# Seam copies ahead of filter units, three fillers fewer, and a gate on one filter load, in a fused Fourier filter and SwiGLU kernel

## The chip, the core, the metric

One core of one Trainium2 chip. The metric is the device time in microseconds (us) of one execution. The kernel before takes 893.56 us (median of 4 runs, 893.45 to 894.48). Ratios below are the mean time of one kernel's runs over that of the other's runs of the same rounds, so they are not quite the ratio of the medians quoted beside them. Later rounds add 40 runs of the kernel before, on the chips of the experiments (892.24 to 898.20).

Engines: PE (matrix multiply; PEld is its weight load), DVE (vector), ACT (scalar), POOL (GpSimd), SP (issues transfers). A "slot" below is one step of the main loop, one of 12 hidden blocks of one group of up to 512 tokens: gate and value matmuls, silu, product, and the down-projection of the block two slots earlier. There are 588. A "filler" is a matmul on zeros whose result nobody uses; a "bank" is one of the buffers (PSUM) into which PE writes and from which the other engines copy; the "opening" is all that comes before the first gate matmul. A "seam" is the slot in which the down-projection of one group ends.

## The reference, cut to what matters

```python
def _attn_ref(x, filt_r, filt_i):          # x: 8 x 3008 x 256
    X = np.fft.rfft(x, axis=1)
    F = (filt_r + 1j * filt_i)[None, :, :]
    return np.fft.irfft(X * F, n=x.shape[1], axis=1)

def _moe_ref(x, w_gate, w_val, w_out, rms_g):   # 24064 tokens, 256 -> 1536 -> 256
    xn = x / rms * rms_g
    g = xn @ w_gate
    return (g * sigmoid(g) * (xn @ w_val)) @ w_out
```

The transform over 3008 = 47 x 64 positions is done with matmuls in two stages, A and B; after stage B the spectrum is multiplied by the real and the imaginary filters; two inverse stages and a norm follow. Batch 0 is transformed in the opening, before the main loop; the other batches' transforms are woven into the main loop, slot by slot.

## The kernel before: the parts concerned

The filters come in four chunks, real (fr) and imaginary (fi). Each chunk is loaded into half of the partitions (f_load) and then copied to the other half (f_dup, by ACT or POOL, in one case by a transfer). The opening, with cuts:

```python
        for c in range(4):
            f_load(c, 0, nc.sync)
            f_load(c, 1, nc.gpsimd if c < 3 else nc.sync)

        warm_up(14, 1)                      # fillers: matmuls on zeros
        for g in range(4):
            wi_group(g)                     # tables for the inverse stage
        for m in range(6):                  # stage A of batch 0
            if m == 4:
                warm_up(6, 0)
            for dh in range(2):
                at_unit(m, dh)
            for g in ((4, 5), (6,), (), (), (7,), ())[m]:
                wi_group(g)
            if m == 4:
                warm_up(3, 0)
        warm_up(2, 0)
        ...
        for g in range(4):
            t1_mm(g)
            t1_copy(g, g == 1)              # token copies: ACT if true, else DVE
        stage_b(0, 1, 2, 3)
        for g in range(4, 8):
            t1_mm(g)
        f_dup(0, 0, A, 0, 2)                # chunk, real/imaginary, engine, rows
        f_dup(0, 1, G, 0, 2)
        f_dup(0, 0, A, 2, 4)
        f_dup(0, 1, G, 2, 8)
        t1_copy(4, 1)
        f_dup(0, 0, A, 4, 8)
        products(0)
        ...
        f_dup(1, 1, G)                      # POOL: the second imaginary chunk
        products(3)                         # POOL's first product, next in its order
```

The main loop emits, per slot, the gate and value matmuls, then the planned units of the next batches, then the down-projection, whose last block ends with the copy of the accumulators (two banks) to SBUF (the seam copy, half on ACT, half on DVE):

```python
        def at(slot, fn, *a):
            todo = {q_unit: late, swap_unit: pre}.get(fn, plan).setdefault(slot, [])
        ...
        for i in range(len(items) + 4):
            for fn, a in pre.get(i, ()):
                fn(*a)
            if i < len(items):
                gv(*items[i])
            for fn, a in plan.get(i, ()):
                fn(*a)
            if 2 <= i < len(items) + 2:
                down(*items[i - 2])         # at i mod 12 = 1: ends with the seam copies
            ...
            for fn, a in late.get(i, ()):
                fn(*a)
```

## Time and profile before

| | before |
|---|---|
| time, median of 4 | 893.56 us |
| span of the profiled execution | 890.6 us |
| PE busy | 873.5 us (98%) |
| first gate matmul (end of the opening) | 47.15 us |
| main loop, from there to the end | 843.45 us |
| visible PE waits in the main loop | 4.3 us |

The lines that carry this are shown in the prediction. One more follows: POOL in the opening of the kernel before. The columns are start, length in us, engine, line, what is written from what, and in brackets the idle time before it and what ended it.

```profile
23.24 1.89 POOL L520 COPY fi<-fi 64x2048 f32<-64x2048 f32 x1 [1.39 <-DMA fi<-in_filt_i_dram]
25.94 1.27 POOL L268 TENSOR_TENSOR sg<-v,fr 128x512 f16<-128x512 f32 x1 [0.81 <-ACT v L266]
27.19 1.26 POOL L269 TENSOR_TENSOR hh<-v,fi 128x512 f16<-128x512 f32 x1
28.51 1.89 POOL L520 COPY fi<-fi 64x2048 f32<-64x2048 f32 x1
30.48 1.27 POOL L268 TENSOR_TENSOR sg<-v,fr 128x512 f16<-128x512 f32 x1
```

The first line is the copy of the second imaginary chunk, which waits for its transfer. After the next wait, for ACT, POOL runs without a gap.

### The profile page before, as it was taken

The numbers are of one execution on the slowest core, as the hardware profiler recorded it, in microseconds if no ns is written. First come the engines' busy times: TensorE is split into PE (matmuls) and PEld (weight loads), VectorE is DVE, ScalarE is ACT, GpSimd is POOL, SyncE is SP. The second block draws the span as 40 slices with busy tenths as digits, with TensorE's granted clock in tenths as the row PEclk, the third lists the DMA queues.
The fourth block names the chain that finished last, engine by engine and source line by source line (L and its number), as shares of the span: only waits on it lengthen the run. The fifth ranks groups of instructions, "written<-read, shape, count | busy, mean of one in ns | idle before, by whom it ended". The sixth has DMA issues, their size and how long they took to land.

```text
span 890.6 us, 17468 instructions
## 1 busy us (share of the span) xinstructions
PE 873.5 (98%) x6258; PEld 559.4 (63%) x6258; DVE 681.5 (77%) x1091; ACT 625.1 (70%) x1068; POOL 435.6 (49%) x392
## 2 busy tenths in 40 slices
PE   8799999999999999999999999999999999999997
PEld 5666666666666666666666666666666666666556
DVE  7866787889987877888688787888878887555555
ACT  7877657677677766877677766787657765676444
POOL 7843830656427661677236662376515762155300
PEclk9999999999999999999999999999999999999999
DMA  8696726675663456335645247233352232222202
GB/s 196 122 196 156 157 67 207 143 158 110 162 159 89 101 111 185 107 90 113 159 119 132 86 81 199 80 94 90 88 163 72 67 90 61 85 66 49 72 24 48
DMA packets 80095, 101.44 MB, mean 114 GB/s; under 512 B 8108, under 2 KB 56684, under 8 KB 79560
## 3 DMA queue, kind: packets, MB, share of 16 engines
q1 hardware_dynamic: 69688, 84.23, 34.8%
q0 software_dynamic: 10240, 15.96, 11.4%
q8 instruction: 49, 0.80, 0.4%
q14 instruction: 38, 0.31, 0.1%
q10 hardware_dynamic: 80, 0.13, 0.1%
HBM read 67.67 MB, written 46.78 MB: 129 GB/s over the span
## 4 chain that ended last, share of the span: by engine, by line
PE 87%; issue 4%; DVE 2%; ACT 2%; DMA 2%; POOL 2%; SPq 0%; ACTq 0%; POOLq 0%; DVEq 0%
PE po L462 26%; PE pg L443 25%; PE pv L443 25%; PE psi L291 3%; PE psb L238 3%; PE psn L323 2%; PE psa L203 2%; DMA fr<-in_filt_r_dram 1%; DVE o L469 1%; ACT fr L516 1%; DVE hh L448 1%; DMA rb<-r_tmp 1%; ACT gT L578 1%; PE psq L352 0%; POOL xc L188 0%
## 5 line engine op out<-in xcount | busy, mean ns | idle before, releaser
L448 DVE TENSOR_TENSOR hh<-pv,sg 128x512 f16<-128x512 f32 (+2 forms) x588 | 392.9, 670 | 190.2 <-ACT sg L447 77.6
L447 ACT ACTIVATE sg<-pg 128x512 f16<-128x512 f32 (+2 forms) x588 | 340.9, 580 | 227.5 <-PE pg L443 217.8
L462 PE MATMUL po<-wo,hh 128*128 128x256 f16 x2244 | 343.2, 272 | 3.8 <-DVE o L469 3.0
L443 PE MATMUL pv<-xn,wv 128*128 128x512 f16 (+2 forms) x1176 | 339.6, 370 | 0.0
L443 PE MATMUL pg<-xn,wg 128*128 128x512 f16 (+2 forms) x1176 | 339.5, 370 | 0.0
L462 PEld LDWEIGHTS <-hh 128*128 128x128 f16 x2256 | 216.4, 98 | 99.0 <-issue 5.3
L282 POOL TENSOR_TENSOR s<-s,s 128x512 f16<-128x512 f16 x102 | 117.9, 1157 | 237.5 <-DVE s L276 165.6
L443 PEld LDWEIGHTS <-wv 128*128 128x128 f16 x1176 | 114.9, 98 | 128.8 <-issue 0.3
L419 POOL TENSOR_TENSOR xn<-y,rb 128x1024 f16<-128x1024 f32 (+1 forms) x45 | 126.0, 2801 | 44.9 <-DMA rb<-r_tmp 37.7
L443 PEld LDWEIGHTS <-wg 128*128 128x128 f16 x1176 | 111.4, 98 | 13.0 <-issue 0.3
L358 POOL TENSOR_TENSOR rho<-u,mhalf 128x4 f32<-128x4 f32 (+1 forms) x48 | 49.1, 1022 | 63.5 <-DVE u L356 63.1
L276 DVE TENSOR_TENSOR s<-psb,fi 64x512 f16<-64x512 f32 x102 | 69.8, 684 | 3.1
L296 ACT ACTIVATE t<-psi 96x512 f16<-96x512 f32 x112 | 66.4, 593 | 8.1 <-PE psi L291 2.7
L278 DVE SCALAR_TENSOR_TENSOR s<-psb,fi 64x512 f16<-64x512 f32 x102 | 70.7, 693 | 1.4
L252 DVE TENSOR_TENSOR s<-psb,fr 128x512 f16<-128x512 f32 x102 | 69.4, 681 | 0.0
L329 ACT ACTIVATE y<-psn,gsb 128x512 f32<-128x512 f32 (+1 forms) x94 | 63.8, 679 | 7.8 <-PE psn L323 0.5
L343 POOL TENSOR_TENSOR sq<-sq 128x512 f16<-128x512 f16 (+1 forms) x35 | 39.6, 1133 | 35.9 <-ACT sq L335 35.9
L335 ACT ACTIVATE sq<-psn 128x512 f16<-128x512 f32 (+1 forms) x94 | 54.8, 583 | 0.0
L208 ACT ACTIVATE t<-psa 128x512 f16<-128x512 f32 x70 | 41.8, 597 | 5.6 <-PE psa L203 2.4
L291 PE MATMUL psi<-s,wi 128*128 128x256 f16 x236 | 44.1, 273 | 0.0
L238 PE MATMUL psb<-t,wb 96*128 96x256 f16 x224 | 43.0, 272 | 0.5 <-DVE s L269 0.5
L323 PEld LDWEIGHTS <-t 128*128 128x128 f16 x368 | 28.4, 98 | 20.6 <-issue 0.4
(104 smaller groups left out, 523.1 us busy)
## 6 DMA issues: line engine op xcount, KB each, us to landing
out_dram<-o SPq DMA_DIRECT2D x83, 256.0 KB
xc<-in_x_dram POOLq DMA_DIRECT2D x56, 192.0 KB, 5.8
z_tmp<-t SPq DMA_DIRECT2D x28, 384.0 KB
t<-z_tmp SPq DMA_DIRECT2D x28, 384.0 KB
g_tmp<-t SPq DMA_DIRECT2D x56, 192.0 KB
rb<-r_tmp SPq DMA_DIRECT2D x41, 256.0 KB
t<-g_tmp SPq DMA_DIRECT2D x21, 384.0 KB
t<-g_tmp SPq DMA_DIRECT2D x7, 320.0 KB
```

The source lines that it names most:

```text
L238: nc.tensor.matmul(ps[:, u, :], w[:, k, :], t, start=True, stop=True)
L252: nc.vector.tensor_tensor(out=s1, in0=ps, in1=f1, op=ALU.mult)
L276: nc.vector.tensor_tensor(out=s2[a], in0=ps[e], in1=f2[e], op=ALU.mult)
L278: nc.vector.scalar_tensor_tensor(out=s2[a], in0=ps[e], scalar=-1.0, in1=f2[e], op0=ALU.mult, op1=ALU.mult)
L282: nc.gpsimd.tensor_tensor(out=s, in0=s1, in1=s2, op=ALU.add)
L291: nc.tensor.matmul(ps[:, u, :], wi_at(q, 2 * i + u), ss[q][:, u, :], start=(q == 0), stop=(q == n - 1))
L296: nc.scalar.activation(out=st[b]["t3"][c][:, 2 * r:2 * r + 2, :], in_=ps[0:KR], func=AXT.Copy)
L419: nc.gpsimd.tensor_tensor(out=xv, in0=yv, in1=rv.unsqueeze(1).to_broadcast([P, 2, n, P]), op=ALU.mult)
L443: nc.tensor.matmul(ps[:, 0:w], wt[:, dt_, ts(jt, P)], xn[:, dt_, :], start=(dt_ == 0), stop=(dt_ == 1))
L447: nc.scalar.activation(out=sg[:, 0:w], in_=pg[:, 0:w], func=AXT.Silu)
L448: nc.vector.tensor_tensor(out=hh[:, 0:w], in0=pv[:, 0:w], in1=sg[:, 0:w], op=ALU.mult)
L462: nc.tensor.matmul(po[s4 // per][:, s4 % per, :], hh[:, ts(s4, P)], wo[:, jt, :], start=(jt == 0 and s4 % per == 0), stop=(jt == JT - 1 an ...
```

## The change

The intent: at a seam, let the copy that frees the accumulator go ahead of the filter units; in the opening, use fewer fillers and keep the transfer queue free for the tokens and the first filters, by letting the second imaginary chunk enter its queue only when stage A of the last tokens has been copied. The token copies are dealt out anew between ACT and DVE. In the main loop, b_unit 15 of batch 1 goes to POOL, and one b_unit and one step of a norm come a slot later. The gate is the new ACT instruction: it writes one zero column into the chunk's tile, so that POOL's load of that tile has to wait for it. The diff, with context cut:

```diff
     def summed(b, i):
-        return b > 1 or b == 1 and i in (6, 7, 10, 11, 14, 15)
+        return b > 1 or b == 1 and i in (6, 7, 10, 11, 14)
 ...
-        if (i in (3, 5, 8, 12)) if b else (i in (3, 7, 9, 12)):
+        if (i in (3, 5, 8, 12, 15)) if b else (i in (3, 7, 9, 12)):
 ...
-        for c in range(4):
-            f_load(c, 0, nc.sync)
-            f_load(c, 1, nc.gpsimd if c < 3 else nc.sync)
+        for e, eng in enumerate((nc.sync, nc.gpsimd)):
+            f_load(0, e, eng)
 ...
-                warm_up(6, 0)
+                warm_up(5, 0)
-            for g in ((4, 5), (6,), (), (), (7,), ())[m]:
+            for g in ((4, 5), (6,), (), (7,), (), ())[m]:
-                warm_up(3, 0)
+                warm_up(1, 0)
         warm_up(2, 0)
+        nc.scalar.activation(out=fi[1][HALF:P, 0, 0:1], in_=mhalf[0:HALF, 0:1], func=AXT.Copy, scale=0.0)
+        for c in range(1, 4):
+            f_load(c, 0, nc.sync)
+            f_load(c, 1, nc.gpsimd if c < 3 else nc.sync)
 ...
-            t1_copy(g, g == 1)
+            t1_copy(g, g % 2)
 ...
+        t1_copy(4, 0)
         f_dup(0, 0, A, 0, 2)
 ...
-        t1_copy(4, 1)
 ...
-            todo = {q_unit: late, swap_unit: pre}.get(fn, plan).setdefault(slot, [])
+            at_seam = slot % JT == 1 and fn in (a_unit, b_unit)
+            todo = late if at_seam or fn == q_unit else pre if fn == swap_unit else plan
+            todo = todo.setdefault(slot, [])
 ...
-                r = (4, 8, 12)
+                r = (5 if (b, m) == (2, 1) else 4, 8, 12)
 ...
-                b_at = [22 + 7 * i // 4 for i in range(16)]
+                b_at = [22 + 7 * i // 4 + (i == 1) for i in range(16)]
```

## The prediction

> **What bounds the kernel now.** I read the page first, for the balance of the engines, and its busy table settles the main stage:
>
> ```profile
> PE 873.5 (98%) x6258; PEld 559.4 (63%) x6258; DVE 681.5 (77%) x1091; ACT 625.1 (70%) x1068; POOL 435.6 (49%) x392
> ```
>
> PE is busy for 98% of the span. The changed lines can then gain in two ways only: where PE visibly waits, and in the opening, where PE is partly busy with fillers or paced by others. So I read next the waits of PE from 47 us (where the gate and value matmuls begin) to the end:
>
> ```profile
> PE po L462 <- DVE o L469: 3.0, 6, 0.8
> PE psb L238 <- DVE s L269: 0.5, 2, 0.3
> PE psq L352 <- POOL sq L343: 0.5, 1, 0.5
> PE po L462 <- DVE hh L448: 0.3, 1, 0.3
> ```
>
> The columns are total us, count and longest. All visible PE waiting in 840 us is 4.3 us, 3.0 of it at the seams between two groups of tokens: the first down-projection matmuls of the next group want the accumulator that DVE has not yet copied out. No change to the order of the main loop can be worth more than this. The timeline of one seam shows why DVE is late:
>
> ```profile
> 88.37 0.68 DVE L268 TENSOR_TENSOR s<-psb,fr 128x512 f16<-128x512 f32 x1
> ...
> 88.97 0.68 DVE L269 TENSOR_TENSOR s<-psb,fi 128x512 f16<-128x512 f32 x1
> ...
> 89.57 0.68 DVE L469 COPY o<-po 128x512 f32<-128x512 f32 x1
> ...
> 90.31 0.38 PE L462 MATMUL po<-wo,hh 128*128 128x256 f16 x2 [0.59 <-DVE o L469]
> ```
>
> Two filter products (b_unit) stand ahead of the seam copy in DVE's order; PE sits idle for 0.59 us. Reading the timeline at each seam gives the others: 0.81 us at 111.59 (two products ahead again), 0.67 at 131.76 (the two swapped products of unit 15, batch 1, come shortly before), 0.30 at 150.87 (one stage A copy ahead) and 0.40 at 165.97 (swapped products of batch 2). The last is not touched by the diff.
>
> Third, the opening, 0 to 47 us, from the timelines of ACT, DVE and POOL. The filter copies on ACT carry the chain of waits there, with DVE close behind:
>
> ```profile
> 20.99 1.16 ACT L516 ACTIVATE fr<-fr 64x512 f32<-64x512 f32 x2 [0.37 <-DMA fr<-in_filt_r_dram]
> 22.17 1.02 ACT L555 ACTIVATE t<-pt 96x1024 f16<-96x1024 f16 x1
> 23.22 1.05 ACT L516 ACTIVATE fr<-fr 64x1024 f32<-64x1024 f32 x1
> 24.30 1.02 ACT L555 ACTIVATE t<-pt 96x1024 f16<-96x1024 f16 x1
> ```
>
> ACT waits for the first real filters, landed at 20.9 us, then two token copies of 1.02 us each stand between its filter copies. DVE starts its products at 21.65 us and ends them at 38.46 us. Its work in between is 12 units x 2 products x 0.60 us (start to start) + 2 copies, 1.27 us, = 15.7 us, so only about 1.1 of the 16.8 us are gaps.
>
> **What the Trainium skill says.** "TensorE: Matmul & The Clock Gate", section "Back-to-back issue gap", gives N/2.4 + 2.5 ns for a warm isolated matmul: 216 ns at 512 columns. The trace agrees: six fillers run from 13.95 to 15.24 us, 215 ns each. For 256 columns it gives 109 ns; four down-projection matmuls from 86.07 to the next start at 86.51 are 110 ns each. "DMA: Bandwidth & Descriptors", section "Issuing engines are not separate DMA queues", says transfers started from different engines run on the same 16 DMA engines and interleave; its section "Queues, rings and completion order" says each DMA engine takes turns between its queues. The trace agrees as far as it goes: with both queues loaded, the DMA share is 0.86 from 14 to 18 us and the last piece of the first real filters needs 8.6 us to land (12.29 to 20.9). Holding back imaginary filters should hence speed the real ones, but moves no byte less.
>
> **The change part by part.**
>
> Seam order: stage A and stage B units at a seam slot (slot mod 12 = 1) are emitted after the last down-projection and its copies. Working through the slot lists, only batch 1's stage A units 9 and 10 (slot 13), its b_units 2 and 9 (slots 25 and 37) and batch 2's last stage A unit (slot 61) are affected; later batches' lists never meet a seam. The seam copy moves ahead by 2 x 0.60 us at slots 25 and 37 and by 0.60 us at slot 61. At 89.57 the copy would start at 88.37 and end at 89.05, before PE wants the bank at about 89.7. So 0.59 + 0.81 + 0.30 = 1.70 us go. The product's matmuls come only 0.4 us later on PE and are ready before DVE has finished the copy, so I expect no new wait.
>
> Unit 15 of batch 1 leaves the summed path for POOL: DVE loses three instructions (0.68 + 0.69 + 0.68 us), two of which delay the seam at 131.76; ACT gains one 0.59 us copy; POOL gives up one 1.16 us sum for two 1.27 us products (it is 26% busy from 120 to 140 us). The gain is the 0.67 us wait. The cost is two more inverse matmuls of 256 columns, 2 x 0.11 = 0.22 us of PE. Net 0.45 us.
>
> Unit 1 of batch 1 one slot later: units 0 and 1 shared one bank in neighbouring slots. It removes the 0.29 us wait of psb at 84.37; the 0.22 us one at 97.13 stays. Third norm step (2,1) one slot later: PE waited 0.49 us at 273.35 for the folded squares, which POOL finished late because a 2.88 us product ran first. A slot is about 2 us, so this wait goes.
>
> Main loop: 1.70 + 0.45 + 0.29 + 0.49 = 2.9 us, all on the path that sets the end, as PE has no other slack there.
>
> Opening: three of 11 fillers in the stage A section go, 3 x 0.215 = 0.65 us, and a group of weight tables moves ahead to cover the wait for the last tokens. The fourth stage-A result, needed at 15.24 us before, would be asked for at about 15.7; the last at about 16.3 rather than 17.01. So the transposes start at 17.4 instead of 18.09 us. But this does not reach the products: ACT now takes the fourth token copy (1.02 us) before the filter copies, so it comes to them at 18.9 + 2 x 1.02 = 20.97 us, as before (20.99). DVE takes the fifth copy before the first product: 21.25 + 0.6 = 21.9 us, 0.25 later than now. What is won is later: ACT has one 1.02 us copy fewer among its filter copies, so most of DVE's 1.1 us of gaps should close. DVE could end at 21.9 + 15.7 = 37.6 instead of 38.46 us; I count 0.5 of this 0.85.
>
> DMA gating: POOL may issue the second imaginary chunk only after ACT's last stage A copy, at about 17.6 us; six issues of about 0.6 us each take it to 21.3 us, where it starts its copy of the first chunk at 19.81 now. The first products need that copy at 22.5 us: it fits, barely. The chunk's landing, 23.2 us now (the POOL copy that waits for it), I expect at 23.5 to 24.5; POOL's first product waits till 25.94 us anyway, for ACT. So I take this as free.
>
> Sum: 2.9 + 0.5 = 3.4 us off 893.5, which is **890.1 us**.
>
> **The rivals.** First: POOL becomes the bound of the opening. From 25.94 to 37.84 us it is busy without a gap, and its last product ends 0.6 us before DVE's. If the gate makes the second imaginary chunk land at 27 us or later, everything in the opening moves by 1 to 2 us, and the gain falls to 1.5 us or so: 892. For it: POOL waited for this very chunk at 23.24 us. Against it: the held-back transfers meet emptier queues. Second: the real filters land at 18 instead of 20.9 us and several steps pull forward together, so that the opening gives back 1 us or more: 889. Against it: DVE's own work is 15.7 us and it starts no earlier. Third: the transfer is hidden anyway, and the opening does not move at all; only the seams count: 890.6. Fourth: the seam fix merely moves the wait to the product's bank or to hh, as the copy and the products are still the same work on DVE. From 80 to 120 us DVE has 1 us idle stretches before many hh products, so there is room; if half came back, 891.5.
>
> **Range and chances.** The main loop's 2.9 us are read off waits, and I give them plus or minus 0.8. The opening may go from 1.0 us better to 1.5 worse than my guess. The runs before lie in 893.45 to 894.48, so a median of few runs may sit some tenths up. I put 8 in 10 on 888.7 to 891.9. Two per cent is 17.9 us, more than four times all visible PE waiting after 47 us; a loss of that size would need a stall that nothing here suggests. So: faster 0.01, same 0.98, slower 0.01.
>
> **What would show it.** The seam waits of PE on the output copy should fall from 3.0 to about 0.6 us, with only that near 163 us (after shifting) left of the large ones; the wait on the folded squares should be gone. In the opening: first transposes at about 17.4 us, first product at 21.9, last DVE product at 37.6 to 38.2, first gate matmul at 46.4 to 46.9 instead of 47.15. Wrong would be: a POOL copy of the second imaginary chunk later than 25.5 us, DVE products that wait on POOL's copies, or new PE waits for psb or hh after the seams.

## The result, and the profile after

The changed kernel takes 891.41 us (median of 4 runs, 890.67 to 891.68) against 893.56 us: 2.15 us less, ratio 0.9972 (95% interval 0.9955 to 0.9990). By the 2% rule that is the same. The time lies inside the predicted range, 1.3 us above the predicted 890.1. But it is put together quite differently, as splitting the profiled span at the first gate matmul shows:

| profiled execution | before | after | difference | predicted |
|---|---|---|---|---|
| opening, to the first gate matmul | 47.15 us | 50.03 us | +2.9 us | -0.5 us |
| main loop, from there to the end | 843.45 us | 839.57 us | -3.9 us | -2.9 us |

The main loop first. This is the answer to the list of PE waits shown in the prediction: the waits of PE after the first gate matmul, in the changed kernel.

```profile
PE po L462 <- DVE o L469: 0.7, 2, 0.4
PE psb L238 <- DVE s L269: 0.2, 1, 0.2
```

The waits for the seam copy went from 3.0 to 0.7 us, the one for the folded squares is gone, and one of two waits for the stage B bank is left, all as predicted. The seam that the prediction showed, now in the timeline of DVE:

```profile
90.14 0.68 DVE L448 TENSOR_TENSOR hh<-pv,sg 128x512 f16<-128x512 f32 x1
90.74 0.68 DVE L469 COPY o<-po 128x512 f32<-128x512 f32 x1
91.33 0.68 DVE L268 TENSOR_TENSOR s<-psb,fr 128x512 f16<-128x512 f32 x1
91.93 0.68 DVE L269 TENSOR_TENSOR s<-psb,fi 128x512 f16<-128x512 f32 x1
```

The copy (L469) stands ahead of the two products now, directly after the hidden product, and DVE does not idle between them.

The opening is the opposite of what was predicted. Four lines of the timeline of POOL, to be read against those of before, and two of DVE:

```profile
18.22 0.54 POOL L503 DMA_DIRECT2D fi<-in_filt_i_dram  x1 [6.36 <-ACT fi L681]
...
21.68 2.04 POOL L520 COPY fi<-fi 64x512 f32<-64x512 f32 x2
26.54 1.89 POOL L520 COPY fi<-fi 64x2048 f32<-64x2048 f32 x1 [2.81 <-DMA fi<-in_filt_i_dram]
28.52 1.27 POOL L268 TENSOR_TENSOR sg<-v,fr 128x512 f16<-128x512 f32 x1
```

```profile
28.46 0.69 DVE L269 TENSOR_TENSOR ss<-psb,fi 128x512 f16<-128x512 f32 x1 [0.72 <-POOL fi L520]
...
33.00 0.69 DVE L269 TENSOR_TENSOR ss<-psb,fi 128x512 f16<-128x512 f32 x1 [0.86 <-POOL fi L520]
```

POOL stands at the gate for 6.36 us, issues the chunk from 18.22 us, and waits for its landing until 26.54 us instead of 23.24. Its first product starts at 28.52 instead of 25.94 us, and DVE now waits for POOL's filter copies, which it did not before. The chain of waits agrees; its columns are start, length and what filled the time:

```profile
17.74 0.21 ACT fi L681
17.95 0.28 issue
18.22 0.54 POOL fi L503
18.76 0.62 POOL fi L506
19.38 7.01 DMA fi<-in_filt_i_dram
26.54 1.90 POOL fi L520
```

It runs through the gate (L681), POOL's issues and 7.01 us of transfer. One more thing differs in the opening, the clock granted to PE, in the table by stretches of 2 us: stretch, its length, busy us (and count) of PE, PEld, DVE, ACT and POOL, then the granted clock, the DMA share and GB/s. First before, then after:

```profile
30.00:32.00 2.00, 1.33 (x16) 1.10 (x17) 1.87 (x4) 1.98 (x4) 1.92 (x3) 1.00 0.58 125
32.00:34.00 2.00, 1.90 (x27) 1.45 (x26) 2.00 (x4) 1.96 (x5) 2.00 (x2) 1.00 0.75 156
```

```profile
30.00:32.00 2.00, 1.03 (x10) 0.84 (x10) 2.00 (x4) 0.72 (x2) 1.94 (x2) 0.50 0.99 205
32.00:34.00 2.00, 2.00 (x15) 1.53 (x13) 0.83 (x2) 1.09 (x3) 1.92 (x2) 0.50 0.00 0
```

After the change PE runs at half clock there; in stretches of 2 us from 28 to 38 us the granted clock is 0.92, 0.50, 0.50, 0.50 and 0.88, which makes 6.8 us at half clock. So there were two suspects for the opening, the gate and the clock, and a third: the new order of the token copies and the fewer fillers.

### The profile page after: what moved, and what is told of

Same layout as the page of the kernel before. It is cut to its first block, busy times and chain, and to the rows that moved or that the text cites. A ratio compares the mean times of both kernels' runs of the same rounds, so it can differ in the third digit from the quotient of the medians. Undisturbed runs are those within 1.5% of the kernel's fastest.

```text
span 889.6 us, 17463 instructions
## 1 busy us (share of the span) xinstructions
PE 875.4 (98%) x6257; PEld 561.5 (63%) x6257; DVE 679.1 (76%) x1088; ACT 625.8 (70%) x1070; POOL 436.5 (49%) x393
## 4 chain that ended last, share of the span: by engine, by line
PE 93%; DMA 2%; DVE 1%; ACT 1%; POOL 1%; issue 1%; POOLq 0%; ACTq 0%
PE po L462 27%; PE pg L443 27%; PE pv L443 27%; PE psi L291 3%; PE psb L238 3%; PE psn L323 2%; PE psa L203 2%; DMA xc<-in_x_dram 1%; DMA fi<-in_filt_i_dram 1%; DVE o L469 1%; PE psq L352 1%; POOL xc L188 0%; PE pt L589 0%; DVE hh L448 0%; ACT gT L578 0%
```

## The experiments

Theory A: the gate delays the second imaginary chunk, POOL carries the whole opening later, and without the gate the change is worth over 4 us. Theory B: the gate is harmless, the copies' order or the fillers cost the opening. Theory C: the drop of the clock costs 1 to 1.5 us by itself.

### 1. The change without its gate

```diff
-        nc.scalar.activation(out=fi[1][HALF:P, 0, 0:1], in_=mhalf[0:HALF, 0:1], func=AXT.Copy, scale=0.0)
```

> The changed kernel without the one ACT instruction that makes the second imaginary chunk wait for stage A; all else as changed. Theory A (the gate lets that chunk land at 26.4 us instead of 23.2, and POOL, which copies it and then works without a gap, carries the whole opening later): POOL's copy of the chunk starts at 23 to 24.5 us, POOL's first product by 26, no drop of the granted clock in the opening, first gate matmul at 46.3 to 47.2 us instead of 50.0, time 887.5 to 889.5 us. Theory B (the new order of token copies or the fewer fillers cost the opening, the gate is harmless): first gate matmul stays at 49.5 to 50.5 and the time at 891 us.

Measured: 888.94 us (888.34 to 890.20, 6 runs) against 893.48 us of before, ratio 0.9945 (0.9925 to 0.9964). First gate matmul at 48.29 us, main loop 839.51 us. POOL in its timeline:

```profile
21.23 1.93 POOL L520 COPY fi<-fi 64x2048 f32<-64x2048 f32 x1 [0.91 <-DMA fi<-in_filt_i_dram]
24.87 1.28 POOL L268 TENSOR_TENSOR sg<-v,fr 128x512 f16<-128x512 f32 x1 [1.71 <-DMA fr<-in_filt_r_dram]
```

The chunk is copied 5.3 us earlier than with the gate and the first product starts 3.65 us earlier. The time is as theory A has it and theory B is out. What A missed: in this profile the first gate matmul came at 48.29, not by 47.2 us, and the clock dropped here too, for a shorter time (3.4 us):

```profile
30.00:32.00 2.00, 1.44 (x9) 1.09 (x10) 1.70 (x3) 1.53 (x4) 2.00 (x3) 0.66 0.63 131
32.00:34.00 2.00, 2.00 (x21) 1.75 (x20) 1.28 (x3) 0.22 (x1) 2.00 (x2) 0.50 0.00 0
34.00:36.00 2.00, 2.00 (x33) 1.85 (x32) 2.00 (x5) 1.98 (x4) 0.36 (x1) 0.99 0.02 8
```

The profile is that of the slowest of the six runs, 890.20 us. The four runs with a mean clock of 0.999 have spans of 886.5 to 886.8 us; less the 839.5 us of the main loop, that is an opening of 47.0 to 47.3 us (an estimate, for the main loop was read in profiles only). So, by the mean clocks, the drop was in two runs of six, and without it A's date was about right.

### 2. The main loop's edits alone, and the opening's alone

The first is the kernel before with these hunks of the change, the second the changed kernel without them:

```diff
-        return b > 1 or b == 1 and i in (6, 7, 10, 11, 14, 15)
+        return b > 1 or b == 1 and i in (6, 7, 10, 11, 14)
-        if (i in (3, 5, 8, 12)) if b else (i in (3, 7, 9, 12)):
+        if (i in (3, 5, 8, 12, 15)) if b else (i in (3, 7, 9, 12)):
-            todo = {q_unit: late, swap_unit: pre}.get(fn, plan).setdefault(slot, [])
+            at_seam = slot % JT == 1 and fn in (a_unit, b_unit)
+            todo = late if at_seam or fn == q_unit else pre if fn == swap_unit else plan
+            todo = todo.setdefault(slot, [])
-                r = (4, 8, 12)
+                r = (5 if (b, m) == (2, 1) else 4, 8, 12)
-                b_at = [22 + 7 * i // 4 for i in range(16)]
+                b_at = [22 + 7 * i // 4 + (i == 1) for i in range(16)]
```

> The kernel before with only the main loop's edits (seam order, unit 15 to POOL, one norm step and one b_unit a slot later). If the two parts of the change simply add, the main loop from the first gate matmul to the end takes 839.6 us as in the changed kernel (843.5 before), and the time is 893.6 - 3.9 = 889.7 us, less than the changed kernel's 891.4. If the loop's gain depended on the opening (a stall shared between them), it is 891 or more.

> The changed kernel's opening with the main loop of before. Theory A: first gate matmul near 50.0 us, main loop 843.5 us, time 893.6 + 1.7 to 2.9 = 895.3 to 896.5 us. If the opening were in truth neutral and only its profile had an unlucky transfer: 893.6 us.

Measured: the main loop's edits alone 890.01 us (888.96 to 890.95, 6 runs), 3.5 us below the 893.48 us of before, ratio 0.9956 (0.9938 to 0.9974), main loop 839.54 us. The opening's edits alone 894.89 us (893.49 to 895.33, 6 runs), 1.4 us above, ratio 1.0008 (0.9990 to 1.0026), main loop 843.43 us. The two add: -3.5 + 1.4 = -2.1, against -2.15 for the whole change. Several things did not come as expected. The opening's cost is below the expected 1.7 to 2.9 us, and its ratio does not exclude zero (one of the 11 runs of before took 898.20 us and raises the mean of before). Its profile, of the fastest of its six runs, has the copy of the second imaginary chunk at 25.20 us and the first gate matmul at 48.27, not near 50. And the profiled execution of the first, whose opening is that of before, has its first gate matmul at 48.86 us, not 47.15, and a drop of the clock from 31 us on. The profiled execution of before, without a drop, had taken 892.44 us, 1.1 us less than the median of 893.56, while that of the changed kernel took 891.47, close to its median. So the profile of before was one of the faster executions, and the +2.9 us between the two profiles overstates what the change does to the opening. The spans of the timed runs, less the main loop of the profiles, give a better estimate: 48.15 us for before (median of the 40 later runs) and 50.0 us for the changed kernel (median of its 9 runs), a difference of 1.9 us.

### 3. The gate alone

The kernel before with the gate and the later loads, and nothing else:

```diff
-        for c in range(4):
-            f_load(c, 0, nc.sync)
-            f_load(c, 1, nc.gpsimd if c < 3 else nc.sync)
+        for e, eng in enumerate((nc.sync, nc.gpsimd)):
+            f_load(0, e, eng)
 ...
         warm_up(2, 0)
+        nc.scalar.activation(out=fi[1][HALF:P, 0, 0:1], in_=mhalf[0:HALF, 0:1], func=AXT.Copy, scale=0.0)
+        for c in range(1, 4):
+            f_load(c, 0, nc.sync)
+            f_load(c, 1, nc.gpsimd if c < 3 else nc.sync)
```

> The kernel before with nothing but the gate and the later place of the loads of chunks 1 to 3 (fillers, token copies and main loop as before). Theory A: the chunk lands late again, POOL's copy of it starts at 26 to 28 us, first gate matmul at 49.5 to 51 us, time 895.5 to 897 us. Theory B: first gate matmul at 47 to 47.5 us and 893.6 us.

Measured: 894.52 us (893.73 to 895.48, 6 runs), 1.0 us above before, ratio 1.0009 (0.9991 to 1.0027), which does not exclude zero. The dates are as expected, the size is not: POOL's copy of the chunk started at 27.00 us and the first gate matmul at 49.94 us, but the time rose by less than the expected 2 us. The expectation counted from the 47.15 us of the fast profile of before; from the 48.86 us that the same opening took in experiment 2, 1.1 us is left. And the profile here is that of the slowest of the six runs (895.48 us).

Set against experiment 1 this also points to an interaction. Without the gate, the other edits of the opening gain 890.01 - 888.94 = 1.1 us (medians; the intervals of the two ratios overlap). With the gate they gain nothing: 894.89 with them, 894.52 without. That fits savings that are not collected when POOL arrives late. Which of these edits saves was not tested: without the gate, the second imaginary chunk also lands 2 us earlier than in the kernel before (copied at 21.23 us against 23.24).

### 4. The gate on another chunk, and the gate later

```diff
-        nc.scalar.activation(out=fi[1][HALF:P, 0, 0:1], in_=mhalf[0:HALF, 0:1], func=AXT.Copy, scale=0.0)
+        nc.scalar.activation(out=fi[2][HALF:P, 0, 0:1], in_=mhalf[0:HALF, 0:1], func=AXT.Copy, scale=0.0)
```

> The changed kernel with the gate on the third imaginary chunk instead of the second. Theory A (the cost of the gate is the late landing of the second chunk): POOL's copy of the second chunk starts by 24 us, first gate matmul at 47 to 48.5 us, time 888.5 to 889.5 us. If it was instead that POOL stands still at the gate and issues late (any gate costs): POOL's copy of the first chunk still begins near 20 us or later, and the time is 890 to 891 us.

In the other kernel the gate and the loads of chunks 1 to 3 stand behind the first four token copies:

```diff
         for g in range(4):
             t1_mm(g)
             t1_copy(g, g % 2)
+        nc.scalar.activation(out=fi[1][HALF:P, 0, 0:1], in_=mhalf[0:HALF, 0:1], func=AXT.Copy, scale=0.0)
+        for c in range(1, 4):
+            f_load(c, 0, nc.sync)
+            f_load(c, 1, nc.gpsimd if c < 3 else nc.sync)
```

> The changed kernel with the gate some 3.5 us later still (after ACT's second token copy, near 21.3 us instead of 17.7). Theory A, as a dose: without the gate 888.9, with it 891.4, and with it 3.5 us later POOL's copy of the second chunk starts at 29 to 31 us, first gate matmul at 52 to 54 us, time 894 to 895.5 us. If the gate's cost were a fixed one (its presence in the queue, not its date): 891.4 us.

Measured, against 893.74 us of before in these rounds: the gate on the third chunk 889.11 us (888.53 to 890.08, 6 runs), ratio 0.9950 (0.9939 to 0.9962); the later gate 896.31 us (895.76 to 896.42, 4 runs), ratio 1.0030 (1.0015 to 1.0045), a little beyond the expected range. POOL's copy of the second chunk with the gate on the third:

```profile
22.65 1.89 POOL L520 COPY fi<-fi 64x2048 f32<-64x2048 f32 x1 [0.33 <-DMA fi<-in_filt_i_dram]
```

Its copies of the first and the second chunk in the later gate's timeline:

```profile
24.95 2.01 POOL L520 COPY fi<-fi 64x512 f32<-64x512 f32 x2
30.89 1.89 POOL L520 COPY fi<-fi 64x2048 f32<-64x2048 f32 x1 [3.92 <-DMA fi<-in_filt_i_dram]
```

| changed kernel, gate | POOL issues the 2nd chunk by | copies it at | first gate matmul | time |
|---|---|---|---|---|
| none | 14.5 us | 21.23 us | 48.29 us | 888.94 us |
| on the third chunk | 15.1 us | 22.65 us | 48.51 us | 889.11 us |
| on the second (as changed) | 20.0 us | 26.54 us | 50.03 us | 891.41 us |
| on the second, later | 23.3 us | 30.89 us | 54.26 us | 896.31 us |

The second column is the end of the chunk's last issue. The first gate matmuls are from one profile each, that of the slowest of six runs in the first two rows and of the fastest of four in the last; the times are the sounder column. A gate as such costs nothing to be seen (889.11 us against 888.94, or ratios to before of 0.9950 and 0.9945); the date of the second chunk does. One sign of the other reading did come: with the gate on the third chunk POOL still stands 2.82 us at it and copies the first chunk at 20.28 us. It did not show in the time. From the last issue to the copy it is 6.7, 7.6, 6.6 and 7.6 us: within the changed kernel, holding the chunk back moved its landing and did not shorten its transfer. In the kernel before there was some gain: 8.5 us without the gate (14.70 to 23.24) and 6.7 us with it (experiment 3, 20.29 to 27.00), 1.8 us faster for an issue 5.6 us later. The later gate also holds the copy of the first chunk back (DVE waits 2.96 us for it), so its last step is not the second chunk's alone.

### 5. The clock in the opening

Two tests with more fillers, on the change without the gate and on the kernel before. A stage B unit of batch 0 has one filler from unit 4 on; here units 5 to 11 have five:

```diff
-        if b == 0 and i > 3:
-            nc.tensor.matmul(ps[:, 0, :], wz[:, 0:P], wz[:, 0:D], start=True, stop=True)
+        for f in range((1 if i < 5 or i > 11 else 5) if b == 0 and i > 3 else 0):
+            nc.tensor.matmul(ps[:, f % 2, :], wz[:, 0:P], wz[:, 0:D], start=True, stop=True)
```

> The kernel of e1_no_gate with four more filler matmuls of 256 columns (0.11 us each) ahead of each stage B unit 5 to 11, so that PE is busier from 24 to 31 us. Theory C (the drop of the granted clock to 0.5 near 30 to 34 us, seen in every profile but that of before, halves PE just when it has to catch up and costs 1 to 1.5 us): no drop of the clock in the opening, DVE no longer idles 1.0 us near 32 us, first gate matmul at 46.5 to 47.2 us instead of 48.3, time 887.5 us. Theory D (the drop is harmless, PE has slack there): the clock stays up and the time stays at 888.9 us, or rises by up to 0.5 us for the fillers' own time.

> The kernel before with the same extra fillers. Theory C: the profile of before without a drop was a lucky execution and most of its timed ones have the drop, so the time falls by about 1 us to 892.4, and its spread narrows. Theory D: 893.5 us, as before, or a little more.

And half the dose, three fillers in units 6 to 9, without the gate:

```diff
-        if b == 0 and i > 3:
-            nc.tensor.matmul(ps[:, 0, :], wz[:, 0:P], wz[:, 0:D], start=True, stop=True)
+        for f in range((3 if 6 <= i <= 9 else 1) if b == 0 and i > 3 else 0):
+            nc.tensor.matmul(ps[:, f % 2, :], wz[:, 0:P], wz[:, 0:D], start=True, stop=True)
```

> The kernel of e1_no_gate with two more filler matmuls (0.11 us each) ahead of stage B units 6 to 9 only, half the dose of e5_warm_no_gate, placed where PE is least busy before the drop of the clock. If the drop costs 1 us and the fillers of e5 merely paid it back with their own time, the clock stays at 0.999 or 1.000, first gate matmul at 46.8 to 47.6 us and the time is 888.0 us, below e1's 888.9. If the drop isn't worth anything that fillers can buy, 888.9 to 889.5 us.

Measured: without the gate and with five fillers 889.46 us (889.00 to 890.46, 6 runs), ratio 0.9955 (0.9943 to 0.9966); the kernel before with five 893.36 us (892.94 to 893.75, 5 runs), ratio 0.9996 (0.9984 to 1.0008); without the gate and with three 889.11 us (888.46 to 890.34, 5 runs), ratio 0.9951 (0.9938 to 0.9965), against 893.74, 893.74 and 893.54 us of before. With five fillers the clock holds: all eleven timed runs have a mean clock of 0.999 or 1.000. With three it holds in four of five. But no time comes back that could be told from noise. One sign of theory C did come, the narrower spread of the kernel before: 0.8 us over 5 runs with the fillers, 3.5 us over the 11 without. Part of the reason for the missing gain is that there was little to gain: of the eleven timed runs without the gate and without added fillers (experiments 1 and 7), six have a mean clock of 0.999 or more anyway. The profile of the first, with the first gate matmul at 47.62 us, shows another part, in one stretch of the table and one line of DVE's timeline:

```profile
30.00:32.00 2.00, 1.74 (x17) 1.38 (x16) 1.59 (x3) 1.98 (x4) 1.82 (x2) 1.00 0.96 201
```

```profile
32.59 0.69 DVE L268 TENSOR_TENSOR ss<-psb,fr 128x512 f16<-128x512 f32 x1 [1.00 <-ACT v L266]
```

The clock stays at 1.00, and DVE idles for 1.00 us near 32 us all the same, as it does, 1.02 us ahead of 32.72, in the kernel without the gate and with the drop. So the five fillers seem to bring a delay of their own. The kernel before shows it more clearly, as neither of its two profiles has the drop; first without the five fillers, then with them:

```profile
31.92 0.69 DVE L268 TENSOR_TENSOR ss<-psb,fr 128x512 f16<-128x512 f32 x1
```

```profile
32.60 0.69 DVE L268 TENSOR_TENSOR ss<-psb,fr 128x512 f16<-128x512 f32 x1 [1.00 <-ACT v L266]
```

With three fillers the profile, of the fastest of its five runs, has neither the drop nor this wait, and the first gate matmul at 47.08 us, about as in the runs without added fillers in which the clock held.

There is a correlation on the other side: of the 40 later runs of before, the 18 with a mean clock of 0.999 or more have a median of 892.57 us and the 22 with 0.998 or less one of 894.05 us. That fits a price of 1.5 us for the drop, but slow transfers may cause both the drop (PE starves) and the time; the profile of the gate on the third chunk has its first gate matmul at 48.51 us with no drop at all. Whether the drop itself costs anything stays open. What is shown: all 9 timed runs of the changed kernel have a low mean clock (0.995 to 0.997), which fits the drop in its profile, and in two kernels without the gate keeping it away with fillers gained nothing. It was not tried in the changed kernel, whose chain of waits runs on PE from 31.07 to 35.5 us, at half clock. So a part of what the gate costs may be paid through the clock; the runs do not say how much.

### 6. The seam order alone

The kernel before with one hunk, one look:

```diff
-            todo = {q_unit: late, swap_unit: pre}.get(fn, plan).setdefault(slot, [])
+            at_seam = slot % JT == 1 and fn in (a_unit, b_unit)
+            todo = late if at_seam or fn == q_unit else pre if fn == swap_unit else plan
+            todo = todo.setdefault(slot, [])
```

> The kernel before with nothing but the seam order (stage A and B units after the seam copies). Read by the start of the first gate matmul of each slot. If each removed wait is worth its idle plus about 0.16 us of pipelined tail, the seams at slots 26, 38 and 62 give 0.6 to 0.75, 0.97 and 0.46 us, a main loop shorter by 2.2 us in all (841.2 instead of 843.45); the waits near 131.8 and 273.4 us stay. If the idle alone counts (0.59 + 0.81 + 0.30), 1.7 us.

Measured: main loop 841.04 us, 2.40 us shorter than before (one timed run, 890.41 us, of unknown state and not used). The differences by slot, read off the starts of the first gate matmul of each slot, for this kernel and for the changed one (the three other profiles with the main loop's edits that were read so agree to 0.02 us); slot 26 is the one in which the next group's down-projection asks for the bank:

| where | seam alone | whole change | idle shown by the profile of before |
|---|---|---|---|
| slot 14, after the seam with stage A units 9 and 10 | -0.17 us | -0.17 us | not read for the prediction |
| slots 23 to 28, b_unit 1 a slot later and the seam at 26 | -0.75 us | -0.99 us | 0.29 + 0.59 us |
| slot 38, seam | -0.98 us | -0.98 us | 0.81 us |
| slots 50 and 52, unit 15 on POOL | 0 | -0.83 + 0.21 us | 0.67 us |
| slot 62, seam | -0.46 us | -0.46 us | 0.30 us |
| slots 143 and 144, norm step | 0 | -0.66 us | 0.49 us |

The sum of the third column is -3.88 us. At each of the four removed seam waits and the norm step, the gain exceeds the idle by 0.16 or 0.17 us (0.75 - 0.59, 0.98 - 0.81, 0.83 - 0.67, 0.46 - 0.30, 0.66 - 0.49). The sixth, b_unit 1, gave 0.99 - 0.75 = 0.24 us for an idle of 0.29, since the unit after it still waits for the bank. The excess fits the pipelined tail of a matmul. A 256-column down-projection matmul is recorded with 272 ns on the mean (in the page: 2244 of them), but back to back they start every 110 ns, so 162 ns of each record lie under the next. When PE stops for a wait, the profile counts idle from the end of the record, and 0.16 us of the stop hide behind it. The Trainium skill, "TensorE: Matmul & The Clock Gate", section "Single matmul latency", gives (398 + N)/2.4 ns for one warm matmul, 272.5 ns at 256 columns, as in the trace. But the ends of matmul records are modelled in these profiles, so this agreement proves little; the starts of the slots, on which the 0.16 us rests, do not depend on it.

### 7. The changed kernel and the one without the gate, on one chip

The kernels of the result and of experiment 1 once more, side by side.

> The changed kernel itself once more, on the same chip and beside the same runs of before as the next one. 891.0 to 891.8 us; POOL's copy of the second imaginary chunk at 25 to 27 us, first gate matmul at 48.5 to 50.1 us (it varies with the landing), main loop 839.6 us.

> The kernel of e1_no_gate once more, for a comparison on one chip: 888.5 to 889.3 us, 2 to 2.7 us below the changed kernel of the same rounds. If the difference of 2.5 us between the two earlier calls was one of chips, it is below 1 us here.

Measured, against 893.40 us of before: the changed kernel 891.80 us (891.10 to 892.42, 5 runs), ratio 0.9983 (0.9971 to 0.9996), first gate matmul at 49.52 us and the copy of the chunk at 26.01 us; without the gate 889.68 us (888.80 to 890.12, 5 runs), ratio 0.9961 (0.9947 to 0.9974), 47.97 and 20.95 us. The first is at the upper end of its expected range and the second 0.4 us above its own, but the difference, 2.1 us, holds and the two ranges do not overlap. **The version without the gate beats both kernels**, by 2.1 to 2.5 us over the changed one and by 3.7 to 4.5 us over the one before (all within the 2% that count as the same).

## Why the prediction was right, and where it was not

The time fell into the range, but by two errors that partly offset each other, which is luck. Both parts lie outside the bounds that the prediction gave them: the main loop gained 3.9 us where it had 2.9 plus or minus 0.8, and the opening lost 1.4 us (experiment 2) to 1.9 us (spans) where it had at worst a loss of 1.0. By its own signs the opening was wrong: the second imaginary chunk was copied later than 25.5 us, and DVE waited on POOL's copies.

- **The list of places in the main loop: right**, except the 0.17 us at slot 14, for which no gain was counted. Every wait that the prediction named went, the one it said would stay stayed, and no new one came (fourth rival: no). The price of unit 15 on POOL was worked out as 0.22 us of PE and measured as 0.21.
- **The size of the main loop's gain: too small.** "1.70 + 0.45 + 0.29 + 0.49 = 2.9 us" measured 3.9. The term that failed is the idle time itself, taken as the price of a wait. Five of the six waits cost 0.16 us more than their idle, 0.8 us together, and slot 14 gives the remaining 0.17.
- **The dates on PE and ACT: nearly right.** The transposes started at 17.77 us (17.4 expected; PE waited 0.17 us for the last tokens with the fillers gone), ACT's filter copies at 21.32 (20.97), the first product at 22.29 (21.9). That the earlier start would not reach the products was right. (Its sum for ACT gives 20.94, not 20.97, and its 21.25 us for the start of DVE's fifth copy stands in no view shown; that copy started at 21.68.)
- **"What is won is later": at most right without the gate.** Instead of the expected 0.5 us, all edits of the opening but the gate gained 1.1 us there (experiments 1 and 2, overlapping intervals), and nothing with the gate. Whether the gain comes from ACT's lighter load, as predicted, was not tested. In the changed kernel DVE's last product ended at 40.83 us, not by 38.2.
- **The gate: wrong, and this is the step that failed.** "The chunk's landing ... I expect at 23.5 to 24.5 ... So I take this as free." It was copied at 26.54 us, and the gate cost 2.1 to 2.5 us in the changed kernel. The dates of POOL's issues were about right (21.68 us for the copy of the first chunk, 21.3 expected). What was not right was a transfer of only 4 to 5 us, on the ground that "the held-back transfers meet emptier queues". The queues were hardly emptier: from 14 to 18 us, with the chunk still held back, the DMA share was 0.81 against 0.86 before, for SP went on issuing the real chunks. The last piece took 7.01 us. The trace of before already had the figure nearer the mark: 8.3 us in the median for these loads.
- **The first rival was the one that came true**, with its mechanism as put there: POOL the bound of the opening, its products late, DVE waiting for its copies. Its threshold, a landing at 27 us or later, was half a microsecond too high. The half clock of PE stood neither in the prediction nor in its rivals.
- **The sum.** Predicted -2.9 - 0.5 = -3.4 us; measured by parts -3.5 + 1.4 = -2.1 in timed runs (medians), -2.15 for the whole.

A last point of method: the prediction took 47.15 us for the end of the opening before, from one execution. It belongs to the faster ones: the two other profiles with exactly that opening, of experiments 6 and 2, have it at 47.52 and 48.86 us. The main loop, by contrast, mostly repeats to within 0.1 us (839.50 to 839.59 us in the seven profiles with all its edits and no added fillers), so its differences can be read off single profiles, slot by slot. An exception is the profile of experiment 3, with 843.76 us, 0.3 us more than the others of its loop, and a wait of PE for tokens that they do not have.

## What to carry to other kernels

Price a wait of PE by its idle plus the pipelined tail of the matmul before it (here 0.16 us), and a held-back transfer by its measured issue-to-landing time under load, not by what an empty queue would do: in the changed kernel, the load that was issued 5.5 us later was copied 5.3 us later. Before gating a load, ask which engine consumes it and whether that engine has any slack after it; here POOL had none, and the rest of the opening's edits, worth 1.1 us without the gate, gained nothing with it. Keep the order of the seam: what frees the buffer that PE asks for next goes first, work for the next batch after it.

## What the Trainium skill lacked or had wrong

- "TensorE: Matmul & The Clock Gate", section "What's actually happening", gives the half clock after at least one idle window of about 3.4 us. Here the clock fell to 0.50 while PE was far from idle: in the kernel without the gate PE was busy for 2.51 of 4 us and 1.35 of 2 us just before (24 to 30 us). The time at half clock fits the page's window: from the table of that kernel (0.66, 0.50, 0.99 in stretches of 2 us) it is 1.36 + 2.00 + 0.04 = 3.4 us, and in the changed kernel 6.8 us, twice that. A later section, "A second HAM failure mode: psum-queue depth-cycling", does tell of drops from frequent short idles, without a figure. How busy is busy enough the page does not say, and busy time in such stretches does not decide it: the kernel before, with 2.48 of 4 us and 1.35 and 1.33 of 2 us from 24 to 32 us, stayed at 1.00.
- "DMA: Bandwidth & Descriptors", section "Anatomy of one DMA — SWDGE (gpsimd) path", has a fit of 2.0 us plus bytes over 436 GB/s for a transfer, about 2.2 us for 96 KB. Under load here, a piece of 96 KB took 7.01 us from issue to landing. The page has no such figure for a GpSimd load beside another busy queue.
- No page says that the idle time that a profile shows before a matmul leaves out the tail of the one before it: 0.16 to 0.17 us at each of five waits here.
